# Where a recurrence's preparation is emitted: between two steps, or behind the first third of a step

## The chip, the cores and the metric

The kernel runs on one core of a Trainium2 chip. The metric is device time in microseconds (us). The kernel before took 978.39 us as the median of three runs (973.5 to 979.82).

## The reference, cut to what matters

Four batches of eight heads, 768 tokens and a head width of 40 go through a recurrence with a 40x40 state per head. Its outputs, one row of 8*40 = 320 numbers per token, go through a feed-forward pair of matrices (320 to 2048 to 320) with a piecewise square between them.

```
for t in range(S):                                   # recurrence, per batch and head
    y[t] = r_t @ state
    Sa   = state @ a_t
    state = state * w_t - outer(Sa, b_t) + outer(v_t, k_t)
h = x @ w_in                                         # x: [3072, 320]
g = where(h >= 1, h, where(h <= -1, 0, (h + 1)**2 / 4))
out = g @ w_out
```

## The kernel before

**Chunks and half-batches.** The 768 tokens are cut into NC = 24 chunks of 32. The 32 heads are split into two half-batches, `hb` 0 and 1, of 16 heads. For each chunk and half-batch the generator `chain(c, hb)` (L454) emits five stages, one per call of `next`. Stage 1 is L468 on TensorE with an eviction on ScalarE (L473). Stage 2 is L479 with evictions on VectorE (L486) and ScalarE (L490). Stage 3 is L497 with evictions on VectorE (L504, L509). Stage 4 is L526 with evictions on ScalarE (L530, L516). Stage 5 is L536 with one on ScalarE (L538). Each stage needs the stage before it, and stage 1 of a chunk needs stages 3 and 5 of the chunk before it.

**Steps.** The main loop (L847) runs ten steps per chunk. A step (L833) emits the next stage of one half-batch and then three times `feed(1024)`, which takes 1024 columns' worth of feed-forward instructions from the generator `moe()` (L571). Behind the first of these thirds come `pull(wgen, 2)` (conversion of the feed-forward's weights, early in the run) and, in the first chunks, a copy to DRAM; behind each third `background(...)` (L366) takes its share of the work for later sets of four chunks. Numbered within a chunk, steps 0, 2, 4, 6 and 8 are stages 1 to 5 of half-batch 0; steps 5, 7 and 9 are stages 1 to 3 of half-batch 1; steps 1 and 3 are stages 4 and 5 of half-batch 1 of the chunk before.

**Preparing the coming chunk.** `load_ti` (L385, through `load_rows`, L274) loads the tokens' rows into one of two buffers, one for each half-batch, with four transfers. `turn` (L416) transposes parts of them on VectorE: part 0 is the pair L423, part 1 is L426, part 2 is L428. `scores` (L430) multiplies the transposed parts, 64 small matmuls (L438) on TensorE, and masks the result with four VectorE instructions (L447). `load_cg` (L390) loads the chunk's other operands with six transfers (L398, L401, L409). All loads are issued from SyncE's queue (SP). A call of `load_ti` overwrites the buffer that `turn` part 2 has just read. Of these calls, `scores(c, 1)` stands between steps 0 and 1 of a chunk; `turn(c+1, 0, .)` before steps 2, 3 and 5, the last with `load_ti(c+2, 0)` behind it; `scores(c+1, 0)` before step 6; and `turn(c+1, 1, .)` before steps 7 and 8 and after step 9, the last with `load_ti(c+2, 1)`.

**Feed-forward.** One block of 128 hidden units and 256 tokens is eight matmuls (L607) into one of two PSUM buffers, a Relu (L613) and a square (L614) on ScalarE, one VectorE instruction (L620) that reads the same PSUM buffer, a rounding on ScalarE (L594), a difference on GpSimd (L595), and six matmuls with the second matrix (L581, L585), which are emitted one block later. In `feed`, a block counts 8*240 + 6*320 = 3840 columns. The feed-forward starts 5 steps after the first 64 tokens are done, and what is left of it runs behind the last chunk.

**Background.** For each set of four chunks, `prelude` (L217) makes scaled rows on VectorE (L239, L240, L243, L249, L252) and GpSimd (L245, L255, L257) and stores them; `ab_set` (L276) transposes them (L287) and multiplies (L298); `invert` (L311) inverts small triangular matrices on GpSimd (L326, L332) and stores the result (L335), which `load_cg` of that set then reads (L409). `WINDOWS` says between which steps each piece is due and `SHARE` how much of it goes to which step of ten.

**What sets the order.** The schedule is written out by hand: every engine runs its instructions in the order in which the program emits them, and semaphores make an instruction wait for its operands. SP's transfers, too, are issued in the order of emission.

Of the kernel before, what the change touches and what calls it, by code (L numbers as in the profile page):

```python
# [49 lines left out]
def rwkv_moe_kernel(ctx: ExitStack, tc: tile.TileContext, r, k, v, w, a, b, w_in, w_out, ident_d, mask_d, out):  # L50
    nc = tc.nc
    S = r.shape[2]
    NC = S // L
# [301 lines left out]
    def drain(key, s):  # L355

        while done.get(key, -1) < s:
            next(back[key])
# [26 lines left out]
    def load_ti(c, hb):  # L385
        drain("rows", c // 4)
        tis[c, hb] = tih[hb]
        load_rows(tih[hb], c, 0, 200, 16 * hb, 16)
# [27 lines left out]
    def turn(c, hb, part):  # L416
        u = 2 * c + hb
        cg, pr = cgs[u % 3], prs[u % 3]
        t5 = tis[c, hb].rearrange("p h (j x) -> p h j x", x=40)[:, :, :, 0:32]
        if part == 0:  # L420
            for f in range(2):
                rows = slice(64 * f, 64 * f + 64)
                nc.vector.transpose(cg[rows, f::2, C_X : C_X + 32], t5[rows, :, 4, :])  # L423
        elif part == 1:
            evs[u] = work.tile([128, 8, 2, 32], F32, tag="ev", name="ev")
            nc.vector.transpose(evs[u], t5[:, :, 1:3, :])  # L426
        else:
            nc.vector.transpose(pr[:, :, :, 8:40], t5[:, :, 0:4:3, :])  # L428

    def scores(c, hb):  # L430
        u = 2 * c + hb
        cg, pr, ev = cgs[u % 3], prs[u % 3], evs.pop(u)
        ps = psum()[:, 0:256].rearrange("p (h x) -> p h x", x=64)
        for k in range(2):
            for p in order:
                for f in range(2):
                    rows = slice(64 * f, 64 * f + D)
                    nc.tensor.matmul(  # L438
                        ps[quarter(f, p // 4), p % 4, 32 * k : 32 * k + 32],
                        lhsT=ev[rows, p, 1 - k, :],  # L440
                        rhs=pr[rows, p, 0, 8:40] if k else cg[rows, 2 * p + f, C_X : C_X + 32],
                        start=True, stop=True,
                    )
        for f in range(2):
            q = slice(64 * (1 - f), 64 * (1 - f) + 32)
            for i in range(2):
                nc.vector.tensor_tensor(  # L447
                    out=cg[q, f::2, C_X : C_X + 64][:, 4 * i : 4 * i + 4].rearrange("p h (j x) -> p h j x", x=32),
                    in0=ps[quarter(f, i)].rearrange("p h (j x) -> p h j x", x=32),
                    in1=mask[quarter(f, i)].unsqueeze(1).unsqueeze(1).broadcast_to([32, 4, 2, 32]),  # L450
                    op=ALU.mult,
                )
# [274 lines left out]
    def pull(gen, n=1):  # L727
        for _ in range(n):
            if next(gen, "end") == "end":
                return False  # L730
        return True
# [91 lines left out]
    def feed(cols):  # L823

        if not Xs:
            return
        owed[0] += cols * (not idle[0])
        while owed[0] > 0:
            d = next(mgen)
            owed[0] = 0 if d is None else owed[0] - d  # L830
            idle[0] = d is None

    def step(c, hb):  # L833

        if (c, hb) in gens:
            next(gens[c, hb], 0)
        for k in range(3):
            if (c, hb) in gens:
                feed(1024)
            if k == 0:  # L840
                pull(wgen, 2)
            if first and k == 0:
                first.pop(0)()
            background(now[0] + (k + 1) / 3)
        now[0] += 1

    for c in range(NC + 1):  # L847
        nxt = c + 1 < NC
        if c < NC:
            gens[c, 0] = chain(c, 0)  # L850
        if nxt:
            load_cg(c + 1, 0)
        step(c, 0)
        if 0 < c < NC:
            scores(c, 1)
        step(c - 1, 1)
        for g, (t0, nt) in enumerate(groups):
            if t0 + nt == 32 * c:
                reclaim(5 + g % 2)
                Xs[g] = relayout(g)  # L860
                if idle[0]:
                    owed[0], idle[0] = -TRAIL * 3072, False
        if nxt:
            turn(c + 1, 0, 0)
        step(c, 0)
        if nxt:
            turn(c + 1, 0, 1)
        step(c - 1, 1)
        if c == NC:
            break  # L870
        step(c, 0)
        if nxt:
            turn(c + 1, 0, 2)
            if c + 2 < NC:
                load_ti(c + 2, 0)
        gens[c, 1] = chain(c, 1)
        if nxt:
            load_cg(c + 1, 1)
        step(c, 1)
        if nxt:  # L880
            scores(c + 1, 0)
        step(c, 0)
        if nxt:
            turn(c + 1, 1, 0)
        step(c, 1)
        if nxt:
            turn(c + 1, 1, 1)
        step(c, 0)
        step(c, 1)
        if nxt:  # L890
            turn(c + 1, 1, 2)
            if c + 2 < NC:
                load_ti(c + 2, 1)
    for _ in mgen:
        pass

# [29 lines left out]
```

## Time and profile before

| | |
|---|---|
| median of the runs shown | 978.39 us (973.5 to 979.82) |
| profiled execution | 976.18 us, span 974.4 us |
| mean granted TensorE clock | 0.85 |
| TensorE matmul busy | 775.0 us (80%) |
| VectorE busy | 590.4 us (61%) |
| ScalarE busy | 478.6 us (49%) |
| GpSimd busy | 443.8 us (46%) |

In the profile's pages PE is TensorE, PEld its weight loads, DVE VectorE, ACT ScalarE, POOL GpSimd and SP SyncE; SPq is SyncE's queue, which issues transfers. L12 is line 12 of the kernel. The profiled execution was 2.2 us shorter than the median of the runs. The matmul busy time counts instructions that overlap, so a busy TensorE is not one at its peak.

### The profile page before, as it was taken

Reading aid. Unit: us, or ns where it says so; the run is one execution under the profiler, and the core shown is the slowest. Engines: PE = TensorE matmul, PEld = TensorE weight load, DVE = VectorE, ACT = ScalarE, POOL = GpSimd, SP = SyncE. Lnnn points to the kernel's source line nnn. Section 1 sums busy time; section 2 is a strip of 40 time slices with the busy share of each in tenths; the row PEclk is TensorE's granted clock in tenths of the full one; section 3 lists DMA queues with packets and bytes.
Section 4 is the critical chain, followed back from the end, with each engine's and each line's share of the span. In section 5 each row is a group of like instructions: output and inputs, shape, how many; then the busy total and the mean of one; then the engine's idle time right before and its main releaser. Section 6 shows DMA issues by size and latency. Waiting matters only on the chain.

```text
span 974.4 us, 35827 instructions
## 1 busy us (share of the span) xinstructions
PE 775.0 (80%) x14976; PEld 692.1 (71%) x14976; DVE 590.4 (61%) x1562; ACT 478.6 (49%) x1230; POOL 443.8 (46%) x673
## 2 busy tenths in 40 slices
PE   4523543447886988799879798989999999999995
PEld 3312532336776887688879687978898899999995
DVE  7782876574756583775654774776665556655321
ACT  5822444212543544454445454546565566656663
POOL 5200223686331599332588232697235962222332
PEclk9755555575997789797999796999999999999998
DMA  8799995565677755896735886856855545552010
GB/s 274 148 193 245 202 207 151 141 139 134 146 156 152 163 138 115 178 186 130 179 100 117 182 160 133 173 135 131 146 115 121 110 101 111 105 90 56 16 36 14
DMA packets 276866, 134.64 MB, mean 138 GB/s; under 512 B 194984, under 2 KB 266856, under 8 KB 276704
## 3 DMA queue, kind: packets, MB, share of 16 engines
q1 hardware_dynamic: 273504, 121.20, 57.9%
q0 software_dynamic: 3200, 11.14, 3.8%
q8 instruction: 118, 1.93, 0.9%
q14 instruction: 44, 0.36, 0.1%
HBM read 96.83 MB, written 33.82 MB: 134 GB/s over the span
## 4 chain that ended last, share of the span: by engine, by line
PE 34%; DMA 16%; POOL 16%; DVE 12%; issue 8%; SPq 8%; ACT 4%; POOLq 0%; ACTq 0%; DVEq 0%
PE ph L607 11%; PE po L581 6%; POOL lw L326 5%; POOL lw L332 4%; DMA ti<-scr 4%; PE po L585 3%; PE p L497 3%; POOL gl L595 3%; SPq L274 3%; PE p L468 3%; PE p L526 2%; DMA ld_a<-in_a_dram 2%; PE p L438 2%; PE p L479 2%; PE p L536 1%
## 5 line engine op out<-in xcount | busy, mean ns | idle before, releaser
L607 PE MATMUL ph<-X,w 120*128 120x256 f32 x1536 | 260.9, 307 | 51.6 <-DVE qt L620 44.3
L595 POOL TENSOR_TENSOR gl<-qt,gh 128x256 fp32r<-128x256 f32 x192 | 140.9, 734 | 280.0 <-ACT gh L594 264.6
L607 PEld LDWEIGHTS ph<-X,w 120*128 120x128 f32 x1536 | 219.8, 203 | 68.1 <-DVE qt L620 51.3
L620 DVE SCALAR_TENSOR_TENSOR qt<-qt,ph 128x256 f32<-128x256 f32 x192 | 79.9, 416 | 150.3 <-ACT qt L614 148.3
L581 PE MATMUL po<-wide,gh 128*128 128x320 f32 x768 | 163.7, 329 | 0.3 <-ACT gh L594 0.3
L594 ACT CAST gh<-qt 128x256 fp32r<-128x256 f32 x192 | 78.0, 406 | 167.6 <-DVE qt L620 166.7
L581 PEld LDWEIGHTS po<-wide,gh 128*128 128x128 f32 x768 | 124.6, 202 | 3.7 <-ACT gh L594 0.5
L613 ACT ACTIVATE qt<-ph,half_c 128x256 f32<-128x256 f32 x192 | 91.1, 474 | 53.4 <-POOL gl L595 39.7
L585 PE MATMUL po<-wide,gl 128*128 128x320 f32 x384 | 99.6, 338 | 17.6 <-POOL gl L595 17.6
L497 PE MATMUL p<-cg 128*64 128x72 f32 (+1 forms) x1536 | 74.8, 262 | 44.2 <-DVE cg L486 39.7
L497 PEld LDWEIGHTS p<-cg 128*64 128x64 f32 x1536 | 66.8, 166 | 54.3 <-ACT cg L490 45.0
L326 POOL TENSOR_TENSOR lw<-lw 128x31 f32<-128x31 f32 (+15 forms) x155 | 94.4, 609 | 18.0 <-DMA lw<-abd 9.3
L490 ACT ACTIVATE cg<-p 32x160 f32<-32x160 f32 x192 | 56.8, 296 | 87.9 <-DVE cg L486 61.0
L447 DVE TENSOR_TENSOR cg<-p,mask 32x256 f32<-32x256 f32 x192 | 80.6, 420 | 25.8 <-PE p L438 23.2
L332 POOL TENSOR_TENSOR lw<-lw 128x31 f32<-128x31 f32 (+15 forms) x155 | 84.1, 543 | 8.8
L504 DVE SCALAR_TENSOR_TENSOR cg<-p,pr 40x160 f32<-40x160 f32 x184 | 59.1, 321 | 41.1 <-PE p L497 39.2
L614 ACT ACTIVATE qt<-qt 128x256 f32<-128x256 f32 x192 | 80.2, 418 | 6.1
L585 PEld LDWEIGHTS po<-wide,gl 128*128 128x128 f32 x384 | 65.6, 197 | 23.9 <-POOL gl L595 21.5
L468 PE MATMUL p<-cg 128*64 128x72 f32 x1536 | 66.4, 243 | 16.7 <-DMA cg<-ttd 15.0
L486 DVE SCALAR_TENSOR_TENSOR cg<-p,mask 32x128 f32<-32x128 f32 x192 | 55.2, 288 | 36.2 <-PE p L479 30.7
L468 PEld LDWEIGHTS p<-cg 128*64 128x64 f32 x1536 | 58.7, 149 | 23.6 <-issue 19.0
L526 PE MATMUL p<-ident,cg 40*64 40x40 f32 x1472 | 57.1, 238 | 1.9 <-issue 1.9
(104 smaller groups left out, 1027.9 us busy)
## 6 DMA issues: line engine op xcount, KB each, us to landing
ti<-scr SPq DMA_DIRECT2D x96, 200.0 KB
ti<-scr SPq DMA_DIRECT2D x96, 168.0 KB
scr<-arena POOLq DMA_DIRECT2D x16, 640.0 KB, 5.4
cg<-scr SPq DMA_DIRECT2D x96, 80.0 KB
X<-Y SPq DMA_DIRECT2D x36, 160.0 KB
scr<-wide SPq DMA_DIRECT2D x8, 640.0 KB
tiab<-scr SPq DMA_DIRECT2D x32, 160.0 KB
scr<-in_r_dram SPq DMA_DIRECT2D x24, 160.0 KB
```

The lines of the kernel that those rows point to most:

```text
L326: eng.tensor_mul(t3, W3[:, 0:n, j : j + 1].broadcast_to([128, n, m]), L3[:, j + 1 :, j].unsqueeze(1).broadcast_to([128, n, m]),)
L332: eng.tensor_sub(W3[:, 0:n, j + 1 :], W3[:, 0:n, j + 1 :], t3)
L447: nc.vector.tensor_tensor(out=cg[q, f::2, C_X : C_X + 64][:, 4 * i : 4 * i + 4].rearrange("p h (j x) -> p h j x", x=32), in0=ps[quarter(f, ...
L468: nc.tensor.matmul(psv[h // 8][64 * (1 - f) : 64 * (1 - f) + 64, h // 2 % 4, 0:72], lhsT=cg[:, h, C_T : C_T + 64], rhs=cg[:, h, C_R : C_R ...
L497: nc.tensor.matmul(psv[h // 8][64 * f : 64 * f + 64, h // 2 % 4, 0:n3], lhsT=cgw[:, h * CW + C_G : h * CW + C_G + 64], rhs=cg[:, h, C_R : ...
L581: nc.tensor.matmul(pos[i], lhsT=gh[:, ts_], rhs=w2[f // 8][:, j, f % 8, :], start=f == 0 and j == 0, stop=False)
L585: nc.tensor.matmul(pos[i], lhsT=gl[:, ts_], rhs=w2[f // 8][:, 0, f % 8, :], start=False, stop=f == NF - 1)
L595: nc.gpsimd.tensor_sub(gl, gt, gh.bitcast(F32))
L607: nc.tensor.matmul(ph, lhsT=w1[:, wi, fs], rhs=Xs[g][:, xi, :], start=i == 0, stop=i == 7)
L613: nc.scalar.activation(gt, ph, AF.Relu, bias=half_c, scale=0.5)
L614: nc.scalar.activation(gt, gt, AF.Square)
L620: nc.vector.scalar_tensor_tensor(out=gt, in0=gt, scalar=1.0, in1=ph, op0=ALU.min, op1=ALU.max)
```

## The change

The calls of `turn`, `scores` and `load_ti` no longer stand between two steps. They are handed to the step that follows them, which emits them once, behind its stage and the first third of its feed-forward, and ahead of `pull(wgen, 2)` and of the step's background. The pair `turn(c+1, 1, 2)`, `load_ti(c+2, 1)`, which stood behind step 9, goes into step 0 of the next chunk. `load_cg` stays where it was, ahead of the step.

```diff
-    def step(c, hb):
+    def step(c, hb, *preparations):
         if (c, hb) in gens:
             next(gens[c, hb], 0)
         for k in range(3):
             if (c, hb) in gens:
                 feed(1024)
             if k == 0:
+                for f, *x in preparations:
+                    if f:
+                        f(*x)
+            if k == 0:
                 pull(wgen, 2)
...
+    left = []
     for c in range(NC + 1):
         nxt = c + 1 < NC
+        if_next = lambda f, *x: (f if nxt else None, *x)
+        more = lambda hb: (load_ti if c + 2 < NC else None, c + 2, hb)
...
-        step(c, 0)
-        if 0 < c < NC:
-            scores(c, 1)
-        step(c - 1, 1)
+        step(c, 0, *left)
+        step(c - 1, 1, (scores if 0 < c < NC else None, c, 1))
...
-        if nxt:
-            turn(c + 1, 0, 0)
-        step(c, 0)
-        if nxt:
-            turn(c + 1, 0, 1)
-        step(c - 1, 1)
+        step(c, 0, if_next(turn, c + 1, 0, 0))
+        step(c - 1, 1, if_next(turn, c + 1, 0, 1))
...
         step(c, 0)
-        if nxt:
-            turn(c + 1, 0, 2)
-            if c + 2 < NC:
-                load_ti(c + 2, 0)
         gens[c, 1] = chain(c, 1)
         if nxt:
             load_cg(c + 1, 1)
+        step(c, 1, if_next(turn, c + 1, 0, 2), more(0))
+        step(c, 0, if_next(scores, c + 1, 0))
+        step(c, 1, if_next(turn, c + 1, 1, 0))
+        step(c, 0, if_next(turn, c + 1, 1, 1))
         step(c, 1)
-        if nxt:
-            scores(c + 1, 0)
-        step(c, 0)
-        if nxt:
-            turn(c + 1, 1, 0)
-        step(c, 1)
-        if nxt:
-            turn(c + 1, 1, 1)
-        step(c, 0)
-        step(c, 1)
-        if nxt:
-            turn(c + 1, 1, 2)
-            if c + 2 < NC:
-                load_ti(c + 2, 1)
+        left = [if_next(turn, c + 1, 1, 2), more(1)]
```

## Rows read from the trace of the kernel before

**Rows 1.** Windows: per stretch each engine's busy us (count), PE clock, DMA share, GB/s.

```profile
240.00:680.00 440.00, 389.13 (x7551) 345.40 (x7551) 281.60 (x803) 208.30 (x555) 237.50 (x364) 0.88 0.70 150
345.00:375.00 30.00, 25.65 (x458) 22.77 (x459) 22.97 (x52) 13.01 (x35) 28.04 (x41) 0.84 0.66 146
...
780.00:910.00 130.00, 130.00 (x2637) 118.10 (x2626) 76.67 (x205) 81.21 (x216) 44.39 (x68) 1.00 0.42 87
```

**Rows 2.** Waits of PE, 240 to 680 us: us in total, times, longest.

```profile
PE ph L607 <- DVE qt L620: 30.6, 12, 6.1
```

**Rows 3.** Timeline, a stall at 275 us: start, us, engine, line; [idle before <-releaser].

```profile
272.25 0.89 DVE L423 STREAM_TRANSPOSE cg<-ti 64x256 f32<-64x256 f32 x2
273.15 1.21 DVE L486 SCALAR_TENSOR_TENSOR cg<-p,mask 32x128 f32<-32x128 f32 x4
...
274.39 0.42 DVE L620 SCALAR_TENSOR_TENSOR qt<-qt,ph 128x256 f32<-128x256 f32 x1
...
274.87 1.22 PE L607 MATMUL ph<-X,w 120*128 120x256 f32 x8 [1.99 <-DVE qt L620]
```

**Rows 4.** Timeline, the last stall of that kind.

```profile
647.67 1.30 PE L607 MATMUL ph<-X,w 120*128 120x256 f32 x8 [2.59 <-DVE qt L620]
```

**Rows 5.** Timeline, SP's queue and VectorE around 170 us.

```profile
168.36 2.34 SPq L274 DMA_DIRECT2D ti<-scr  x4
...
170.81 0.39 SPq L398 DMA_DIRECT2D cg<-scr  x1
...
172.72 0.94 SPq L409 DMA_DIRECT2D cg<-ttd  x2
173.71 0.64 SPq L225 DMA_DIRECT2D ld_w<-in_w_dram  x1
...
176.46 0.18 DVE L237 TENSOR_SCALAR arena<-ld_w 128x40 f32<-128x40 f32 x1 [5.99 <-DMA ld_w<-in_w_dram]
```

**Rows 6.** Timeline, SP's queue and VectorE around 238 us.

```profile
234.12 0.35 SPq L335 DMA_DIRECT2D ttd<-lw  x1
236.76 0.80 SPq L409 DMA_DIRECT2D cg<-ttd  x2
...
242.26 0.20 DVE L239 TENSOR_TENSOR arena<-ld_a,arena 128x40 f32<-128x40 f32 x1 [12.06 <-DMA ld_a<-in_a_dram]
```

**Rows 7.** Timeline, PE and DVE in a half-chunk without background.

```profile
839.54 1.22 PE L497 MATMUL p<-cg 128*64 128x72 f32 x32
...
845.46 0.48 PE L438 MATMUL p<-pr,ev 40*32 40x32 f32 x32
845.87 1.13 PE L526 MATMUL p<-ident,cg 40*64 40x40 f32 x32
845.99 1.72 DVE L447 TENSOR_TENSOR cg<-p,mask 32x256 f32<-32x256 f32 x4 [1.75 <-PE p L438]
846.93 0.74 PE L607 MATMUL ph<-X,w 120*128 120x256 f32 x4
847.51 0.75 PE L581 MATMUL po<-wide,gh 128*128 128x320 f32 x4
847.72 0.89 DVE L423 STREAM_TRANSPOSE cg<-ti 64x256 f32<-64x256 f32 x2
...
850.54 0.42 DVE L620 SCALAR_TENSOR_TENSOR qt<-qt,ph 128x256 f32<-128x256 f32 x1
...
851.99 1.11 PE L607 MATMUL ph<-X,w 120*128 120x256 f32 x8
...
853.32 0.90 PE L497 MATMUL p<-cg 128*64 128x72 f32 x21
```

**Rows 8.** Waits of VectorE, 240 to 680 us.

```profile
DVE cg L447 <- PE p L438: 9.8, 8, 2.2
```

**Rows 9.** Chain of waits around 730 us: start, us, what.

```profile
730.55 8.80 DMA ti<-scr
```

**Rows 10.** Waits over the whole span.

```profile
PE p L497 <- DVE cg L486: 39.7, 4, 19.1
```

## The prediction

> **What bounds the kernel now.** I read the windows first, then the waits, then the timeline at the waits. The windows [rows 1] show three regimes. From 780 to 910 us TensorE is busy for all of 130 us at a granted clock of 1.00: there only its own work counts, and the change neither adds nor removes any, so that stretch and the tail stay as they are. From 240 to 680 us it is busy 389.1 of 440 us at a mean clock of 0.88: 50.9 us are idle, and the clock takes at most another 0.12 * 440 = 52.8 us. That is where the order of emission can win or lose. The 345-to-375 stretch is one of three (two more begin at 480 and 630) in which GpSimd is busy nearly throughout, 28.04 of 30 us here. The start, before 240 us, is loads, conversions and background; its views come with the parts below.
>
> Of the 50.9 us, 30.6 are waits of L607 for L620 [rows 2], because L620 frees one of the two PSUM buffers. The timeline shows what kept VectorE from it: the pair L423 takes 0.89 us, then L486 1.21, then L620, and 0.06 us after L620's end the matmuls start, 1.99 us late [rows 3]. Eight stalls between 240 and 680 us read so, with L423, L486 and L620 back to back; the last is at 647.67 [rows 4]. L423 is what the change moves. Its row shows no wait of its own, so it sits there only because of where it was emitted.
>
> **Transposes.** What they cost does not change, only their place in VectorE's queue. A block of feed-forward counts 8*240 + 6*320 = 3840 columns and a step feeds 3*1024 = 3072, so L620 falls at four fixed places in five steps. Walking `moe()` through, these are the first third of steps 2 and 7, the first third of 3 and 8, the second third of 4 and 9, and the last third of 5 and 0. Therefore L423, emitted before steps 2 and 7, comes behind both L486 and L620 of that step, L426 behind the L620 of steps 3 and 8, and L428 keeps its place between its neighbours, since stage 1 puts nothing on VectorE. In each of the eight stalls L620 can end 0.89 us sooner. Three of the eight lie in the stretches in which GpSimd is full [rows 1]; there it is late next (its L595 feeds L585), and I count nothing. The other five give 5 * 0.89 = 4.5 us; the bounds are 0 and 8 * 0.89 = 7.1.
>
> **Clock.** Idle time is paid again in the clock: 52.8 us lost beside 50.9 idle [rows 1], at most 1.04 us for each us of idle removed. Its lower end is 0, since some stalls stay long enough. I take the whole, 4.5 us, since every stall that shrinks lies in the window of that row.
>
> **No feed-forward yet.** Before 190 us L497 waits 39.7 us for L486 in four pieces [rows 10], each with L423 ahead: 4 * 0.89 = 3.6 us at best. But weight conversions stand in VectorE's queue around them, and behind L486 the same L423 is still in front of the next conversion. What is gained at L497 is owed there. I take 0, and keep 3.6 as the end.
>
> **SP's queue.** `load_ti` waits for L428 and blocks what is behind it. Today `load_cg` is behind it; afterwards `load_cg` goes first and can use that wait. Around 168 us the four issues of `load_ti` begin when L428 ends, then `load_cg` takes from 170.81 to 173.66, and only then comes ld_w, for which VectorE idles 5.99 us [rows 5]. Ld_w could be issued 2.9 us sooner. Its landing took 2.75 us from issue to L237 behind a queue of `load_ti` data, so I take 2 of the 2.9. At 238 us the swap does harm: there SP stands before L335 (issued at 234.12, when GpSimd's inversion was done) and then L409, and VectorE idles 12.06 us for the next loads [rows 6]. Today `load_ti` has been issued ahead of that wait; afterwards its four issues, 2.34 us [rows 5], come between L409 and ld_w. The bound is 3 us, with its data on the engines; I take 2.3. Net about 0, between -2.9 and +3. The loads `load_ti` makes are used seven steps later; a half-chunk of five steps lasts 853.32 - 839.54 = 13.78 us [rows 7], so 19.3 us against a landing of at most 8.80 [rows 9]. A delay of a third of a step and a stage is covered.
>
> The Trainium skill, in "DMA: Bandwidth & Descriptors", section "Issuing engines are not separate DMA queues", says that issue time on a sequencer is usually small beside the transfer itself. By it the swap at 168 us would be worth about nothing, and this part would come to +2.3 instead of 0; here the six issues of `load_cg` took 2.85 us and ld_w's transfer 2.75, so the row does not bear it out.
>
> **Scores.** TensorE now does L526 (1.06 us until the next start) and four L607 (0.58 us) ahead of L438, so L447, which waits for L438, starts 1.64 us later when VectorE was already waiting: it idled 1.75 us there [rows 7]. Queued behind L447 are the step's background and then L486 and L620 of the next step. L423 no longer stands between, so the net delay of that L620 is at most 1.64 - 0.89 = 0.75 us. In the quiet half-chunk L620 ends at 850.96 and TensorE needs it at 851.99 [rows 7], a margin of 1.03 us, and it is free. With more than 1.03 - 0.75 = 0.28 us of VectorE background in steps 1 and 2, or 6 and 7, it begins to bite. In the stretch from 240 to 680 us VectorE waits at L447 in 8 half-chunks [rows 8]; the price lies between 0 and 8 * 0.75 = 6 us, before the clock. I take 1, being nearer to the quiet row: elsewhere VectorE arrives late and the wait is not there. L526 itself is emitted earlier by the 64 matmuls of scores; its consumers come two steps later, so nothing is gained. Scores still come nearly four steps ahead of stage 1.
>
> **Sum.** -4.5 - 4.5 + 0 + 1 = -8. Against the profiled execution's own 976.2 us that is 968.2; that execution lay 2.2 us below the median of 978.4, on whose scale it is 970.4. I give 970. With each term between a third and its whole, this case's own range is 965 to 976.
>
> **Rivals.**
> 1. *Another queue is late next* (about 977). If GpSimd and the loads set the pace wherever VectorE is late, the 0.89 us turn into waits for L595 or for a load. For it: GpSimd's 28.04 of 30 us, and waits for loads like those of [rows 5, 6]. Against it: in the five counted stalls TensorE starts the moment L620 ends. It leaves -1 us or so.
> 2. *It does more than the sum* (about 960). All eight stalls shrink, 7.1 us, the clock gives as much again, 7.4, and SP's gain at 168 us stays whole without the loss at 238, 2.9: together 17.4, so 961 on the median's scale. For it: idle time and slow clock stand about one to one in [rows 1]. Against it: rival 1's reasons.
> 3. *Slower: VectorE is held at L447* (about 989). The place is step 1 or 6; each time VectorE arrives before L438 it stands until TensorE has run a stage and a third, with the background behind it. If that takes hold in 16 half-chunks, twice those of [rows 8], it costs 16 * 0.75 = 12 us and the clock again as much, 24, less about half the forecast's -9 and what rival 1 hides; around +11. It decides from 0.28 us of background behind L447 on. For it: [rows 8] has VectorE early in 8 of them already. Against it: at the long stalls VectorE was late, not early, so the halves that lose are those with most margin.
>
> The Trainium skill, in "Perfetto Trace Analysis", section "Per-engine timelines", says of VectorE, ScalarE and GpSimd that their queues are strictly first in, first out, so that a wait holds up whatever follows. That speaks against the change, by way of the third rival, and the trace agrees: L423, whose data lay ready, stood behind L447's 1.75 us of idle [rows 7].
>
> **How the numbers follow.** Forecast 0.38, another queue 0.25, more than the sum 0.22, slower 0.15. One per cent of 978.4, about what a measurement can tell from no change, puts the limits at 968.6 and 988.2. Faster: rival 2 and the lower third of the forecast, 0.22 + 0.14 = 0.36. Slower: most of rival 3, 0.13. Same: the rest, 0.51. The range runs from 957, a little below rival 2, to 986, which leaves out the upper part of rival 3 (0.12) and a tail of 0.07 below.
>
> **What would show it.** In the profile after, L620 should follow L486 directly with L423 behind it, and the waits of L607 for L620 should fall from 30.6 us by about 5, with a mean clock above 0.88 in the same stretch. L447's waits for L438 should grow from 9.8 us by about 1.6 per case; if L607's waits for L620 rise with them, rival 3 has it. If L607's waits fall and L585's waits for L595 or VectorE's waits for loads grow by as much, it is rival 1. SP's `load_cg` should be issued ahead of `load_ti`, and ld_w near 171 us. The forecast is wrong if the time before 240 us moves by more than 4 us, or if the windows behind 780 us are no longer full.

## The result, and the profile after

The change made the kernel slower by 0.6 per cent. Its median is 981.89 us over 20 runs (976.47 to 985.31), that of the kernel before on the same chips 976.67 us over 20 runs (969.91 to 986.21): a ratio of 1.0058, with a 95% interval of 1.0038 to 1.0079. (Ratios, here and below, are taken over the runs, and differ a little from the quotients of the medians, 1.0053 here.) A run more than 1.5 per cent above the fastest of its kernel is left out of ratios and means. Forecast were 970 us and a ratio below 1; the time lies inside the range of 957 to 986, on the other side of no change. The profiled execution took 981.62 us with a span of 979.8 us, against 976.18 and 974.4 before.

The windows of the kernel after answer to [rows 1] (columns as there):

```profile
240.00:680.00 440.00, 389.60 (x7411) 343.06 (x7410) 275.30 (x799) 204.75 (x549) 236.67 (x363) 0.88 0.68 148
345.00:375.00 30.00, 28.33 (x469) 24.64 (x469) 21.53 (x51) 12.23 (x34) 28.11 (x41) 0.75 0.60 133
780.00:910.00 130.00, 130.00 (x2562) 117.06 (x2562) 75.48 (x204) 77.22 (x207) 44.07 (x68) 0.97 0.41 92
...
780.00:790.00 10.00, 10.00 (x129) 8.89 (x129) 5.19 (x15) 4.97 (x15) 9.29 (x17) 0.67 0.40 84
```

TensorE is as busy between 240 and 680 us as before (389.6 against 389.1 us) at the same 0.88, and full behind 780 us; its clock there is below 1.00 only in the first 10 us. Over the whole of the 440 us nothing shows a loss. Two shorter stretches have a lower clock: 345 to 375 us (0.75 against 0.84, with TensorE busier, 28.33 against 25.65 us) and 780 to 790 us (0.67; 780 to 910 was at 1.00 before). The waits of TensorE in the same 440 us answer to [rows 2]:

```profile
PE ph L607 <- DVE qt L620: 18.4, 8, 6.1
PE po L585 <- POOL gl L595: 15.7, 11, 3.6
PE ph L607 <- DMA X<-Y: 9.0, 6, 4.1
PE p L298 <- DVE ea L287: 4.1, 1, 4.1
PE p L298 <- DVE yt L509: 2.6, 1, 2.6
```

L607's waits for L620 fell by 12.2 us, from 30.6 to 18.4, more than forecast. Other waits took their place: before, L585 waited 9.5 us for L595, L607 5.1 us for the relayout's loads (X<-Y, which bring the feed-forward its tokens), and L298 1.8 us for L287 and not at all for L509. These grew by 6.2, 3.9, 2.3 and 2.6 us, 15.0 in all. The stall of [rows 3] shows one such exchange in the timeline of the kernel after, VectorE and TensorE together:

```profile
269.50 1.21 DVE L486 SCALAR_TENSOR_TENSOR cg<-p,mask 32x128 f32<-32x128 f32 x4
270.74 0.42 DVE L620 SCALAR_TENSOR_TENSOR qt<-qt,ph 128x256 f32<-128x256 f32 x1
271.08 0.90 DVE L423 STREAM_TRANSPOSE cg<-ti 64x256 f32<-64x256 f32 x2
...
276.79 1.42 DVE L287 STREAM_TRANSPOSE ea<-tiab 128x256 f32<-128x256 f32 x4 [3.22 <-DMA tiab<-scr]
...
279.89 0.85 PE L298 MATMUL p<-ea 40*32 40x32 f32 x64 [2.64 <-DVE yt L509]
```

L423 now follows L620, and the 1.99 us of [rows 3] are gone. Some 8 us later VectorE stands 3.22 us for a load, L509 is late behind it, and TensorE waits 2.64 us.

VectorE's waits answer to [rows 8] and [rows 6]:

```profile
DVE cg L447 <- PE p L438: 39.7, 17, 6.5
DVE arena L239 <- DMA ld_a<-in_a_dram: 22.2, 5, 15.2
```

L447 is held in 17 half-chunks, not 8, and the wait for ld_a at 242 us grew from 12.06 to 15.20 us. SP's queue and VectorE, in the timeline of the kernel after, answer to [rows 5]:

```profile
161.36 0.94 SPq L409 DMA_DIRECT2D cg<-ttd  x2
165.34 2.92 SPq L274 DMA_DIRECT2D ti<-scr  x4
168.30 0.64 SPq L225 DMA_DIRECT2D ld_w<-in_w_dram  x1
...
171.78 0.18 DVE L237 TENSOR_SCALAR arena<-ld_w 128x40 f32<-128x40 f32 x1 [4.34 <-DMA ld_w<-in_w_dram]
...
241.85 0.20 DVE L239 TENSOR_TENSOR arena<-ld_a,arena 128x40 f32<-128x40 f32 x1 [15.20 <-DMA ld_a<-in_a_dram]
```

`load_cg` goes ahead of `load_ti`, and the wait for ld_w falls from 5.99 to 4.34 us; with turns and loads alone it is 3.87, with the loads alone 4.09, and with the turns alone, where `load_ti` stays ahead, 5.77. (The stretch as a whole comes earlier too: half-chunk (1, 1), before it, starts at 155.21 instead of 159.17 us.)

The quiet half-chunk of [rows 7] shows a loss that no wait shows. The timeline of the kernel after, the same half-chunk (20, 1):

```profile
844.08 1.22 PE L497 MATMUL p<-cg 128*64 128x72 f32 x32
...
849.16 0.64 PE L607 MATMUL ph<-X,w 120*128 120x256 f32 x4
849.73 1.13 PE L526 MATMUL p<-ident,cg 40*64 40x40 f32 x32
850.79 0.73 PE L607 MATMUL ph<-X,w 120*128 120x256 f32 x4
851.45 0.46 PE L438 MATMUL p<-cg,ev 40*32 40x32 f32 x32
851.73 0.48 PE L438 MATMUL p<-pr,ev 40*32 40x32 f32 x32
852.14 0.85 PE L581 MATMUL po<-wide,gh 128*128 128x320 f32 x4
852.83 0.46 PE L585 MATMUL po<-wide,gl 128*128 128x320 f32 x2
853.21 0.70 PE L479 MATMUL p<-x,cg 32*32 32x72 f32 x32
...
858.05 0.72 PE L497 MATMUL p<-cg 128*64 128x72 f32 x16
```

And of the kernel before, the rows around those of [rows 7]:

```profile
844.62 0.64 PE L607 MATMUL ph<-X,w 120*128 120x256 f32 x4
...
848.09 0.46 PE L585 MATMUL po<-wide,gl 128*128 128x320 f32 x2
848.48 0.70 PE L479 MATMUL p<-x,cg 32*32 32x72 f32 x32
```

From the first four L607 to L479 the same matmuls take 848.48 - 844.62 = 3.86 us before and 853.21 - 849.16 = 4.05 us after, without a wait and at full clock. The half-chunk grew by as much: 858.05 - 844.08 = 13.97 against 13.78 us. Before, L438 and L526 stand together, one trip of TensorE from the feed-forward to small matmuls and back; after, there are two. Four L607 ahead of L438 take 0.66 us to its start (850.79 to 851.45), where the same four took 0.58 before, to the start of L581 [rows 7]. Four L581 behind L438 take 0.69 (852.14 to 852.83), where behind L607 they took 0.58 (847.51 to 848.09).

### The profile page after: what moved, and what is told of

It is laid out like the page before. It is cut to its first block, busy times and chain, and to the rows that moved or that the text cites. A ratio compares the mean times of both kernels' runs of the same rounds, so it can differ in the third digit from the quotient of the medians.

```text
span 979.8 us, 35875 instructions
## 1 busy us (share of the span) xinstructions
PE 787.4 (80%) x14976; PEld 699.1 (71%) x14976; DVE 585.8 (60%) x1562; ACT 476.0 (49%) x1230; POOL 443.9 (45%) x673
## 4 chain that ended last, share of the span: by engine, by line
PE 38%; DMA 14%; DVE 13%; SPq 12%; POOL 11%; issue 6%; ACT 4%; ACTq 0%; DVEq 0%; POOLq 0%
PE ph L607 12%; PE po L581 7%; POOL lw L326 4%; PE po L585 4%; POOL lw L332 3%; PE p L497 3%; SPq L274 3%; PE p L468 3%; PE p L526 2%; DMA ld_a<-in_a_dram 2%; PE p L438 2%; DVE cg L447 2%; DMA tiab<-scr 2%; DMA X<-in_moe_w_in_dram 2%; SPq L558 2%
## 5 line engine op out<-in xcount | busy, mean ns | idle before, releaser
L607 PE MATMUL ph<-X,w 120*128 120x256 f32 x1536 | 262.9, 308 | 41.7 <-DVE qt L620 30.9
L595 POOL TENSOR_TENSOR gl<-qt,gh 128x256 fp32r<-128x256 f32 x192 | 140.9, 734 | 282.5 <-ACT gh L594 269.0
L607 PEld LDWEIGHTS ph<-X,w 120*128 120x128 f32 x1536 | 221.4, 204 | 58.7 <-DVE qt L620 41.1
L581 PE MATMUL po<-wide,gh 128*128 128x320 f32 x768 | 169.7, 338 | 0.3 <-ACT gh L594 0.3
L620 DVE SCALAR_TENSOR_TENSOR qt<-qt,ph 128x256 f32<-128x256 f32 x192 | 79.9, 416 | 133.1 <-ACT qt L614 131.1
L447 DVE TENSOR_TENSOR cg<-p,mask 32x256 f32<-32x256 f32 x192 | 80.6, 420 | 89.6 <-PE p L438 81.6
L581 PEld LDWEIGHTS po<-wide,gh 128*128 128x128 f32 x768 | 125.4, 204 | 5.3 <-ACT gh L594 0.5
L585 PE MATMUL po<-wide,gl 128*128 128x320 f32 x384 | 100.2, 339 | 25.7 <-POOL gl L595 25.6
L490 ACT ACTIVATE cg<-p 32x160 f32<-32x160 f32 x192 | 56.6, 295 | 98.1 <-PE p L479 52.8
L497 PE MATMUL p<-cg 128*64 128x72 f32 (+1 forms) x1536 | 70.3, 252 | 39.3 <-DVE cg L486 32.4
L326 POOL TENSOR_TENSOR lw<-lw 128x31 f32<-128x31 f32 (+15 forms) x155 | 94.1, 607 | 16.1 <-DMA lw<-abd 7.4
L497 PEld LDWEIGHTS p<-cg 128*64 128x64 f32 x1536 | 62.6, 157 | 48.9 <-ACT cg L490 40.1
L585 PEld LDWEIGHTS po<-wide,gl 128*128 128x128 f32 x384 | 66.4, 199 | 31.9 <-POOL gl L595 29.6
L332 POOL TENSOR_TENSOR lw<-lw 128x31 f32<-128x31 f32 (+15 forms) x155 | 83.9, 541 | 8.8
L468 PEld LDWEIGHTS p<-cg 128*64 128x64 f32 x1536 | 59.7, 150 | 24.9 <-issue 19.5
L526 PE MATMUL p<-ident,cg 40*64 40x40 f32 x1472 | 59.1, 243 | 12.4 <-ACT x L473 6.7
L526 PEld LDWEIGHTS p<-ident,cg 40*64 40x64 f32 x1472 | 53.5, 151 | 18.9 <-ACT x L473 6.9
```

The costliest lines, as they stand in the source:

```text
L326: eng.tensor_mul(t3, W3[:, 0:n, j : j + 1].broadcast_to([128, n, m]), L3[:, j + 1 :, j].unsqueeze(1).broadcast_to([128, n, m]),)
L332: eng.tensor_sub(W3[:, 0:n, j + 1 :], W3[:, 0:n, j + 1 :], t3)
L447: nc.vector.tensor_tensor(out=cg[q, f::2, C_X : C_X + 64][:, 4 * i : 4 * i + 4].rearrange("p h (j x) -> p h j x", x=32), in0=ps[quarter(f, ...
L468: nc.tensor.matmul(psv[h // 8][64 * (1 - f) : 64 * (1 - f) + 64, h // 2 % 4, 0:72], lhsT=cg[:, h, C_T : C_T + 64], rhs=cg[:, h, C_R : C_R ...
L497: nc.tensor.matmul(psv[h // 8][64 * f : 64 * f + 64, h // 2 % 4, 0:n3], lhsT=cgw[:, h * CW + C_G : h * CW + C_G + 64], rhs=cg[:, h, C_R : ...
L526: nc.tensor.matmul(pst[64 * f : 64 * f + 64, p, :], lhsT=cn[er[f], h, C_S : C_S + 64], rhs=ident[er[f]], start=True, stop=True)
```

## The experiments

Fifteen kernels were run, each held against the kernel before on the same chip. Where two of them are held against each other, the ratio is that of their two ratios, and its interval their two intervals combined as independent errors. A quiet half-chunk is the time between two starts of L497 behind 800 us; before it is 13.72 us in most half-chunks.

### Where the scores are emitted

**Scores alone** behind the first third; turns and token loads stay.

```diff
-        if nxt:
-            scores(c + 1, 0)
-        step(c, 0)
+        step(c, 0, (c + 1, 0) if nxt else None)   # emitted behind feed(1024), k == 0
...
```

> Only scores moves behind the first third; turn and load_ti stay between the steps. Switch theory (TensorE loses about 0.19 us each time it leaves the feed-forward's matmuls for a group of small ones and comes back, and the change adds one such trip per half-chunk): quiet half-chunks behind 800 us last 13.9 us instead of 13.7, 46 trips cost about 9 us, and without the early gains of the other moves the ratio is 1.008 to 1.011. Hold theory (VectorE standing at L447 until L438 is done makes L486 and L620 late): quiet half-chunks stay at 13.7 us, since L620 has 1 us of margin there; waits of L607 for L620 between 240 and 680 us rise above 30.6 us; ratio 1.005 to 1.015.

Measured: 983.21 us, ratio 1.0073 (1.0046 to 1.0100), quiet half-chunks 13.91 us. The scores alone cost about as much as the whole change does (1.0058, 1.0038 to 1.0079). L607's waits for L620 between 240 and 680 us are 30.2 us, as before (30.6). Two of its quiet half-chunks take 14.69 us. There VectorE is held 2.26 us at L447, L423 (still in its old place) follows, then L486 and L620, and the next L620 comes too late:

```profile
849.93 0.51 PE L607 MATMUL ph<-X,w 120*128 120x256 f32 x2 [0.57 <-DVE qt L620]
```

So part of this run's cost is the hold that the prediction described, on top of TensorE's own 0.19 us. With the turns moved as well, no quiet half-chunk shows such a wait.

**Scores directly behind the stage**, ahead of the first third; turns and token loads moved as in the change.

```diff
             next(gens[c, hb], 0)
+        if score:
+            scores(*score)
         for k in range(3):
...
```

> As the changed kernel, but scores is emitted directly behind the stage, ahead of the first third: L526, then L438, then the feed-forward, so the small matmuls stand together again, while L447 still waits 1.06 us longer than before (behind L526). Switch theory: quiet half-chunks of 13.7 us, ratio 0.992 to 0.998, about that of the run with turns and loads alone. Hold theory: between the changed kernel and the run with turns and loads alone, since L447 keeps 1.06 of the 1.64 us: ratio 1.000 to 1.004.

Measured: 980.22 us, ratio 1.0034 (1.0011 to 1.0057), quiet half-chunks 13.73 us. TensorE is back to one trip, and the 0.19 us are gone. L447 still starts a stage later than before (13 waits for L438 between 240 and 680 us, 28.7 us), at no cost that shows against turns and loads alone (below, 1.0032).

**Scores in two parts**, behind the first and the second third, so three trips.

```diff
         for k in range(2):
+            if k:
+                yield
             for p in order:
...
```

> As the changed kernel, but the two halves of scores' matmuls are emitted behind the first and the second third, the masks behind the second half: one more trip of TensorE per half-chunk. Switch theory: quiet half-chunks of 13.92 + 0.19 = 14.1 us, 46 * 0.19 = 9 us more than the changed kernel, ratio 1.013 to 1.018. Hold theory: quiet half-chunks stay where the changed kernel has them or move only where L620 is awaited, since L447 comes about 1 us later still: ratio 1.008 to 1.015, with more waits of L607 for L620.

Measured: 987.71 us, ratio 1.0126 (1.0083 to 1.0169), most quiet half-chunks 14.21 us: another 0.30 us for another trip.

**Masks late**: the score matmuls where the kernel before has them, the masks L447 behind the first third; turns and token loads moved.

```diff
+        yield          # matmuls L438 ahead of the stage; what follows behind feed(1024), k == 0
         for f in range(2):
             q = slice(64 * (1 - f), 64 * (1 - f) + 32)
...
```

> Turns and token loads as in the change; the 32 groups of score matmuls (L438) stand where the kernel before has them, ahead of the step's stage, and only their four masks (L447 on VectorE) go behind the first third. Theory of the trip of TensorE: quiet half-chunks 13.72 us and the time of turns and loads alone, ratio 1.000 to 1.005. Theory that what counts is where the masks stand in VectorE's queue: ratio 1.006 or above, L607's waits for L620 above 32 us.

Measured: 981.52 us, ratio 1.0039 (1.0015 to 1.0064), quiet half-chunks 13.72 us, L607's waits for L620 29.1 us. That is the time of turns and loads alone (below), and of scores behind the stage. By the quiet half-chunks it is TensorE's second trip that the place of the scores costs there, not where the masks stand in VectorE's queue. In the time of the whole kernel the step from these three to the change is not clear of noise by itself: the change's ratio over theirs is 1.0026 (0.9991 to 1.0061), 1.0024 (0.9993 to 1.0055) and 1.0019 (0.9987 to 1.0051).

### Turns and token loads

**Turns and loads alone**; the scores stay between the steps.

```diff
-        step(c - 1, 1, (scores if 0 < c < NC else None, c, 1))
+        if 0 < c < NC:
+            scores(c, 1)
+        step(c - 1, 1)
...
-        step(c, 0, if_next(scores, c + 1, 0))
+        if nxt:
+            scores(c + 1, 0)
+        step(c, 0)
```

> Turn and load_ti move behind the first third, scores stays between the steps. Switch theory: quiet half-chunks of 13.7 us, the early gain of 3 to 4 us before 240 us stays, and the waits of L607 for L620 fall: ratio 0.992 to 0.998. Hold theory: the same direction, ratio 0.990 to 0.998, so this run tells only whether the moved transposes and loads are the harm: if the ratio is above 1.002, both theories are wrong.

Measured: 980.39 us, ratio 1.0032 (1.0004 to 1.0060), quiet half-chunks 13.72 us. This fell on the other side of what was expected: the part of the change that was to bring 9 us costs 3 without any second trip. In its trace the 7th half-chunk (3, 0) starts 4.4 us ahead of the kernel before, the 31st, (15, 0), 0.95 us behind it. Nor does this trace show the gain for which L423 was moved. The waits of TensorE for L620 between 240 and 680 us, and the window:

```profile
PE ph L607 <- DVE qt L620: 31.8, 12, 4.9
```

```profile
240.00:680.00 440.00, 385.75 (x7504) 342.88 (x7504) 279.70 (x801) 206.49 (x553) 237.28 (x364) 0.87 0.68 148
```

L607 waits 31.8 us for L620, against 30.6 before, and TensorE is idle 54.2 us, against 50.9 [rows 1].

**Loads alone.**

```diff
             turn(c + 1, 0, 2)
-            if c + 2 < NC:
-                load_ti(c + 2, 0)
...
-        step(c, 1)
+        step(c, 1, (c + 2, 0) if c + 2 < NC else None)   # load_ti behind feed(1024), k == 0
```

> Only the token loads (load_ti) go behind the first third, with load_cg now ahead of them on SyncE's queue; turns and scores stand where the kernel before has them. Theory SP order: this alone brings both the early gain (ahead of the kernel before by 3 to 4.5 us at the 7th half-chunk, near 240 us) and the loss behind the boundary of a set, where the loads stand behind L335's store (VectorE's wait for ld_a at 241 us 15 us, not 12.1): ratio 1.002 to 1.005, as for turns and loads together. Theory that the turns are what costs: early gain kept, ratio 0.995 to 0.999. Quiet half-chunks 13.72 us by both.

Measured: 978.07 us, ratio 1.0006 (0.9976 to 1.0036). Half-chunk (3, 0) starts 3.3 us ahead and VectorE's wait for ld_a is 15.3 us, as with turns and loads together, but the whole is no slower than before. L607's waits for L620 are 38.9 us in its trace, though no L423 moved: a single trace's sum of these waits moves by several us for other reasons.

**Turns alone**, parts 0 and 1 (L423, L426).

```diff
-        if nxt:
-            turn(c + 1, 0, 0)
-        step(c, 0)
+        step(c, 0, (c + 1, 0, 0) if nxt else None)   # turn behind feed(1024), k == 0
...
```

> Only parts 0 and 1 of the turns (L423, L426) go behind the first third; part 2, the token loads and the scores stay. This is the prediction's term for the transposes by itself. Prediction: L607's waits for L620 between 240 and 680 us fall from 30.6 by about 4.5, no early gain at 240 us, ratio 0.991 to 0.996. Theory that another queue is late next: those waits fall or stay, waits for L595 or loads grow by as much, ratio 0.998 to 1.002. Theory that the turns are what costs: ratio 1.002 to 1.005. Quiet half-chunks 13.72 us by all.

Measured: 980.89 us, ratio 1.0023 (0.9989 to 1.0058), quiet half-chunks 13.72 us: not the 0.991 to 0.996 that the prediction's term gave. In its trace the waits fell by 5.8 us, about as that term had it, and in the sum over the stretch no wait took their place. The waits of TensorE, 240 to 680 us, and the window:

```profile
PE ph L607 <- DVE qt L620: 24.8, 10, 5.4
PE po L585 <- POOL gl L595: 9.0, 11, 2.4
```

```profile
240.00:680.00 440.00, 394.65 (x7526) 350.46 (x7523) 280.35 (x803) 208.44 (x555) 237.56 (x364) 0.86 0.69 148
```

TensorE is idle 45.4 us, 5.5 less than in [rows 1], and its clock is 0.86, not 0.88. Two places show this. First the windows (columns as in [rows 1]) in half-chunk (3, 0), of the kernel before:

```profile
244.00:248.00 4.00, 3.04 (x45) 2.83 (x46) 3.71 (x13) 1.30 (x3) 1.81 (x3) 1.00 0.15 43
248.00:252.00 4.00, 2.65 (x103) 2.21 (x101) 2.62 (x8) 1.80 (x5) 2.12 (x3) 1.00 0.13 28
252.00:256.00 4.00, 4.00 (x62) 3.52 (x58) 3.80 (x12) 3.01 (x9) 2.36 (x3) 1.00 1.14 240
```

and of the kernel with the turns alone moved:

```profile
244.00:248.00 4.00, 2.59 (x72) 2.12 (x70) 3.29 (x12) 1.14 (x4) 1.53 (x2) 1.00 0.14 38
248.00:252.00 4.00, 4.00 (x74) 3.88 (x63) 2.10 (x5) 2.49 (x7) 3.28 (x5) 0.56 0.91 191
252.00:256.00 4.00, 4.00 (x45) 3.47 (x45) 1.91 (x6) 1.68 (x6) 0.00 (x0) 0.50 1.00 247
256.00:260.00 4.00, 4.00 (x44) 3.60 (x44) 1.49 (x4) 2.61 (x7) 0.73 (x1) 0.50 0.69 127
```

The kernel before stalls twice here, and stays at full clock; with one stall left, TensorE runs at the lower level for some 13 us. Second, near 650 us. The kernel before (timeline, then windows):

```profile
656.25 0.56 PE L585 MATMUL po<-wide,gl 128*128 128x320 f32 x2 [0.72 <-POOL gl L595]
```

```profile
650.00:652.00 2.00, 2.00 (x30) 1.85 (x27) 0.95 (x3) 0.87 (x2) 1.35 (x2) 0.50 0.23 75
...
656.00:658.00 2.00, 1.75 (x74) 1.58 (x74) 0.38 (x1) 0.89 (x2) 1.84 (x4) 1.00 0.86 235
```

and the kernel with the turns alone moved:

```profile
643.80 1.61 PE L607 MATMUL ph<-X,w 120*128 120x256 f32 x8 [1.58 <-DVE qt L620]
...
653.30 0.56 PE L585 MATMUL po<-wide,gl 128*128 128x320 f32 x2 [1.62 <-POOL gl L595]
```

```profile
656.00:658.00 2.00, 2.00 (x25) 1.92 (x24) 0.91 (x3) 0.73 (x2) 1.84 (x4) 0.50 1.37 185
...
664.00:666.00 2.00, 2.00 (x39) 1.96 (x40) 1.04 (x2) 0.81 (x3) 1.92 (x4) 0.78 0.00 0
```

Before, TensorE stands 2.59 us for L620 [rows 4] and then 0.72 us for GpSimd's L595. With L423 out of the way the first stall is 1.01 us shorter and the second 0.90 us longer, and behind it TensorE runs at 0.50 for some 10 us, from 655 to 665. Half-chunk (14, 0) takes 20.83 us instead of 16.05.

### GpSimd's load

**The subtractions of the later sets' inversions (L332) left out**: in the kernel before, in turns and loads alone, and in the whole change.

```diff
-            eng.tensor_sub(W3[:, 0:n, j + 1 :], W3[:, 0:n, j + 1 :], t3)
+            if not s:
+                eng.tensor_sub(W3[:, 0:n, j + 1 :], W3[:, 0:n, j + 1 :], t3)
```

> The kernel before with the subtractions of the later sets' inversions (L332 on GpSimd, about 50 us between 240 and 680 us) left out, so that GpSimd is late less often; everything else issues in the same order. It is the base for the next run. If GpSimd's lateness costs TensorE only its 9.5 us of waits for L595 and the clock behind them, ratio 0.980 to 0.992; if GpSimd is nowhere on the path, 0.998 to 1.002.

> Turns and token loads behind the first third, scores as before, with the same subtractions left out; its time is to be held against the kernel before with them left out. Theory that GpSimd takes the gain: with it freed the gain comes out, and this run is 0.3 to 0.8 per cent faster than its base. Theory SP order (or that the turns cost by themselves): it stays 0.2 to 0.5 per cent slower than its base.

> The whole change, with the subtractions of the later sets' inversions (L332) left out; its time is to be held against the kernel before with them left out (947.0 us, 0.9706 of the kernel before) and against turns and loads alone with them left out (942.4 us, 0.9636). Theory of the trip of TensorE (0.19 us in each of 45 half-chunks): 6 to 9 us above the latter, so ratio 0.970 to 0.973, and quiet half-chunks 13.91 us. Theory that only GpSimd's lateness made the change a loss: as fast as the latter, ratio 0.962 to 0.966.

Measured: 947.01 us, 0.9706 (0.9661 to 0.9752); 942.40 us, 0.9636 (0.9589 to 0.9683); 949.47 us, 0.9698 (0.9663 to 0.9734). The base gained far more than expected. On its whole page of groups the kernel before has

```profile
L332 POOL TENSOR_TENSOR lw<-lw 128x31 f32<-128x31 f32 (+15 forms) x155 | 84.1, 543 | 8.8
```

and leaving these 84.1 us of GpSimd out brought 978.76 - 947.01 = 31.8 us. Not all of it need come through TensorE's waits for L595. In the trace of this run the inversion for the second set of chunks also ends sooner (the edit adds a line, so L336 is L335):

```profile
223.74 0.45 SPq L336 DMA_DIRECT2D ttd<-lw  x1
...
235.12 0.20 DVE L239 TENSOR_TENSOR arena<-ld_a,arena 128x40 f32<-128x40 f32 x1 [6.89 <-DMA ld_a<-in_a_dram]
```

Its store is issued 10.4 us earlier than in [rows 6], VectorE's wait for the loads behind it is 6.89 us, not 12.06, and half-chunk (3, 0) starts 7.6 us ahead. How the 31.8 us divide between this way, through SP's queue, and L595 was not tested.

With GpSimd lightened, turns and loads come out ahead of their base, 0.9636 / 0.9706 = 0.993 (0.986 to 1.000). The whole change loses against them, 0.9698 / 0.9636 = 1.006 (1.000 to 1.013), or 7.1 us between the medians (of runs on two chips), with quiet half-chunks of 13.91 against 13.72 us. Against the kernel before with L332 left out the whole change is at 0.999 (0.993 to 1.005).

**The multiplications (L326) left out as well**, in the same three.

```diff
-            eng.tensor_mul(t3, ...)
+            if not s:
+                eng.tensor_mul(t3, ...)
```

> The kernel before with both instructions of the later sets' inversions (L326 and L332) left out, stores and order kept, so that GpSimd has only the differences, roundings and scaled rows. The base for the two runs beside it. By the 31 us that L332 alone brought, and with what is left of GpSimd's lateness, ratio 0.935 to 0.965.

> Turns and token loads behind the first third, scores as before, the same left out; held against its base without the change. Theory that GpSimd takes the gain: 0.4 to 0.9 per cent faster than its base, as with L332 alone left out (0.7). Theory that the turns and loads cost by themselves, or by the clock whatever GpSimd does: 0 to 0.5 per cent slower than its base.

> The whole change, the same left out; held against turns and loads alone with the same left out. Theory of the trip of TensorE: 6 to 9 us slower than that one (as with L332 alone left out, 7), quiet half-chunks 13.91 us; against its base without the change between 0.3 per cent faster and 0.4 slower. Theory without the trip: no slower than turns and loads alone.

Measured: 937.77 us, 0.9579 (0.9530 to 0.9628); 936.16 us, 0.9556 (0.9504 to 0.9609); 941.15 us, 0.9617 (0.9571 to 0.9663). Turns and loads against their base: 0.998 (0.990 to 1.005), less than expected and not told from nothing. The scores' place comes to 941.15 - 936.16 = 5.0 us, in the ratios 1.006 (0.999 to 1.014), with quiet half-chunks of 13.91 us; against the base the whole change is at 1.004 (0.997 to 1.011).

**L595 on VectorE while an inversion is due**, nothing left out: in the kernel before, and in turns and loads alone.

```diff
-            nc.gpsimd.tensor_sub(gl, gt, gh.bitcast(F32))
+            inverting = any(a <= now[0] < b for a, b in WINDOWS["inv"])
+            (nc.vector if inverting else nc.gpsimd).tensor_sub(gl, gt, gh.bitcast(F32))
```

> The kernel before, with the difference L595 on VectorE instead of GpSimd while an inversion is due, nothing left out. Some 25 differences of 0.73 us leave GpSimd, 18 us; by the 31 us that 50 us less of L332 brought, that is worth some 11 us, against at most 25 * 0.5 us more work for VectorE. Theory that GpSimd is on the path in those stretches: ratio 0.986 to 0.997. Theory that VectorE is as tight: 0.998 to 1.006.

> Turns and token loads behind the first third, scores as before, with the difference L595 on VectorE while an inversion is due; to be held against the kernel before with the same. Theory that GpSimd takes the gain: 0.2 to 0.8 per cent faster than that one. Theory that turns and loads cost by themselves: 0.2 to 0.5 per cent slower.

Measured: 963.20 us, 0.9837 (0.9805 to 0.9869); 964.55 us, 0.9865 (0.9830 to 0.9900). The first is a version that beats both kernels, by 14 us the kernel before. In its trace 75 of the 192 differences left GpSimd, not the 25 expected. Its waits of TensorE from 231 to 668 us (the edit adds a line, so L608 is L607 and L621 is L620):

```profile
PE ph L608 <- DVE qt L621: 41.8, 14, 7.0
```

TensorE's waits for the difference are gone from the list, and those for L620 have grown from 30.6 to 41.8 us: VectorE now carries the work. Turns and loads on top of it are 1.003 (0.998 to 1.008): no gain of theirs shows where VectorE got more to do.

## Why the prediction was wrong

Every run lists its span and the mean clock granted over it. Their product is the span at full clock; the rest of the span is counted here as lost to the clock. Means over the runs, us, with 95% half-widths (for before, over the 77 runs made of it beside the experiments):

| kernel | runs | mean clock | lost to the clock | span less that |
|---|---|---|---|---|
| before | 77 | 0.8462 | 150.1 (1.4) | 826.1 (1.1) |
| after | 20 | 0.8414 | 155.3 (2.3) | 824.3 (2.3) |
| scores alone | 11 | 0.8465 | 150.7 (3.1) | 830.9 (3.0) |
| scores in two parts | 6 | 0.8462 | 151.8 (3.4) | 835.0 (4.5) |
| loads alone | 12 | 0.8478 | 148.7 (3.7) | 828.2 (3.6) |
| turns alone | 12 | 0.8412 | 155.4 (4.8) | 823.1 (3.1) |
| turns and loads | 12 | 0.8427 | 153.9 (4.0) | 824.6 (2.6) |
| the same, scores behind the stage | 12 | 0.8427 | 153.8 (3.4) | 824.1 (2.6) |
| the same, masks late | 12 | 0.8382 | 158.6 (3.4) | 821.5 (3.4) |

Of the six kernels whose turns are moved five have the lower clock; scores in two parts, with six runs, has that of the three whose turns stay. The six together lose 5.1 us (1.8) more to the clock than those three.

Such a loss is not so much time. Among the 77 runs of the kernel before, 1 us more lost goes with 0.35 us (0.10) more span, and so with 0.65 us less in the last column. By this the 5.1 us are an estimated 2 us of time, and the 1.5 to 4.6 us by which the last column is lower in five kernels with moved turns are no gain by themselves. More than half of the loss lies where TensorE is idle for more than half of the time (windows of the kernel before, columns as in [rows 1]):

```profile
0.00:100.00 100.00, 38.76 (x906) 29.41 (x909) 67.91 (x147) 47.08 (x101) 19.49 (x28) 0.71 0.87 213
100.00:240.00 140.00, 67.60 (x1360) 61.08 (x1358) 92.43 (x218) 49.19 (x121) 71.66 (x109) 0.60 0.71 161
```

Before 240 us the clock takes 0.29 * 100 + 0.40 * 140 = 85 us, of 974.4 * (1 - 0.85) = 146 in this execution.

**"Transposes" (-4.5): the order came, the time did not.** L620 follows L486 with L423 behind it, and L607's waits for L620 fell by 12.2 us in the change and by 5.8 with the turns alone. But in the change TensorE is idle 50.4 us between 240 and 680 us, against 50.9 before: other waits took the place of the shorter ones. With turns and loads alone it is idle 54.2 us. Only with the turns alone is it idle less, 45.4 us, and even that run measured 1.0023 where this term forecast 0.991 to 0.996.

**"Clock" (-4.5): the step that failed, by its sign.** "Idle time is paid again in the clock" was read from a sum over 440 us, 50.9 us idle beside 52.8 lost. Nothing was paid back: in that stretch the clock is 0.88 in the change, as before, and 0.86 with the turns alone, where idle time did fall. Over the runs the loss is 5.2 us larger in the change and 3.7 to 8.5 in four other kernels with moved turns (1.7 in scores in two parts), where the prediction had 4.5 less. The traces show how it can be: the place and length of the stall that is left matter, not the sum. Fewer stalls at 244 to 252 us left TensorE at 0.50 where two had left it at 1.00; where one stall was 1.01 us shorter, at 643.80 us, the next one was 0.90 us longer, and the half-chunk behind it 4.8 us. In the pairs with GpSimd relieved the loss differs by 135.6 - 134.9 = 0.7 us (L332 out; 5 and 6 runs, half-widths of 9.1 and 6.1), 138.0 - 133.3 = 4.7 (both out) and 151.1 - 144.1 = 7.0 us (L595 on VectorE), always the higher one with the turns moved.

**"Scores" (+1): mis-sized, and sought in the wrong place.** The prediction priced VectorE's wait at L447, and said of the full stretch that "the change neither adds nor removes any" work. The wait came as told, 17 half-chunks. Where the turns are moved it cost nothing measurable (scores behind the stage, with 28.7 us of it, against turns and loads, with 13.1); with the scores alone it reached TensorE in two quiet half-chunks. TensorE's own time grew by 0.19 us in each half-chunk: the sum of the trip's ends, +0.08 in and +0.11 out. Some 40 half-chunks beside feed-forward make at most 40 * 0.19 = 7.6 us. Measured: 983.21 - 977.32 = 5.9 us alone (the kernel before beside it had 977.32), 7.1 and 5.0 in the pairs with GpSimd lightened, and 0.0026 * 977 = 2.5 us between the ratios of the change and of turns and loads, of which the first is clear of no change, the second barely, and the other two are not.

**"SP's queue" (0): right.** The wait for ld_w fell by 1.65 us (2 forecast), that for ld_a grew by 3.1 (2.3 forecast), and the loads alone came to 1.0006. The Trainium skill, in "DMA: Bandwidth & Descriptors", section "Issuing engines are not separate DMA queues", which holds issue time small beside the transfer, would have left the wait for ld_w as it was; as far as one trace goes, the 1.65 us speak against it here.

**"No feed-forward yet" (0)**: L497's waits for L486 before 190 us fell from 39.7 us in 4 to 32.4 in 3, but that is in the same stretch as the earlier ld_w, and was not tested by itself. In the trace after half-chunk (2, 1), at 210 us before, starts 5.9 us ahead and (3, 0), at 241 us, 3.6 us ahead; by (6, 0), at 359 us, nothing of it is left. The prediction had named more than 4 us there as a sign that it was wrong.

**The rivals.** The first, another queue late next, is what the lists of waits show, and the prediction's own sign for it: L595, the relayout's loads, L287 and L509 took over all of the 12.2 us that L620 gave up. It had the gain shrink to nothing, not turn. The third did give the side, but not the mechanism: L447 was held twice as often, as it supposed, and L607's waits for L620 fell. The Trainium skill's rule of strictly first in, first out, in "Perfetto Trace Analysis", section "Per-engine timelines", holds in the trace: L620 at 270.74 us no longer stands behind L423, and L509 at 279.45 us stands behind L287's 3.22 us. It did not decide the sign.

**By size:** turns and loads +3.1 to +3.8 us (ratios of 1.0032 to 1.0039 in three kernels) where -9 was forecast for the transposes and the clock, and the scores' place the rest, some +2 to +2.5, where +1 was; with the scores moved alone it was more, 5.9. That 981.89 us still lies inside the range is owed to its width, which held both signs.

**Open.** Why the spells at the lower clock grow when L423 moves is shown in two places of single traces, not explained; the runs show only that the mean clock is lower. As an estimated 2 us of time it is also not all of the +3. And whether it is GpSimd's lateness that takes the gain of the turns isn't settled: of the three pairs in which GpSimd was relieved one is a gain (0.993), one is nothing (0.998), and one, where VectorE took the work, a loss (1.003), with intervals that overlap.

## What to carry to other kernels

Do not credit a shorter stall with time, and again with clock, before you have looked at each place for the stall that TensorE reaches next; count a loss if that one gets longer. Where TensorE is full, the order of its own instructions is a cost: keep small matmuls beside other small ones, since each further trip from the large ones and back cost 0.19 to 0.30 us here. And price an engine by leaving some of its work out: GpSimd, busy 46% of the span, gave back 31.8 us for 84.1 us of its work, which no list of TensorE's waits for it had shown (L585's idle time before L595's results is 17.6 us over the whole span); in part it may have come through the loads that stand behind GpSimd's result.

## What the runs showed of the hardware

A trip of TensorE between large feed-forward matmuls and the small ones costs time by itself, with no wait in the trace: 0.19 us for a second one in a half-chunk (13.91 against 13.72 us), 0.49 us for the second and third (14.21 us). After a stall the clock can stay at 0.50 (1.2 GHz) for about 10 us of unbroken work, as from 655 to 665 us with the turns alone moved, and behind the stall of 2.59 us that ended at 647.67 it was back at 1.00 (2.4 GHz) by 654 us in the kernel before. Behind one stall of 1.41 us, with the turns alone moved, TensorE was at 0.50 from 248 to 262 us; behind two of 1.37 and 1.35 us, in the kernel before, it stayed at 1.00. So stalls of like length are followed by spells of very different length, and two executions of one kernel differ by more than the change is worth (969.9 to 986.2 us for the kernel before).
